# Attention and two mixtures on one core: the probability-value matmuls of a pair in two adjoining visits, with a padded last key chunk

## The chip, the cores and the metric

The kernel runs on one core of one Trainium2 chip. The metric is device time in microseconds (us): the median over runs, and beside it one execution that the hardware profiler recorded. TensorE (PE in the rows) multiplies matrices and transposes; VectorE (DVE), ScalarE (ACT) and GpSimd (POOL) do the rest; SyncE (SP) issues the loads. Each engine works through its own queue in order, and waits on semaphores for the others.

## The reference

Only the first of its three stages matters here, a block-causal attention over 4 batches, 8 heads, 576 positions of 64 values:

```python
scores = scale * np.matmul(q, k.transpose(0, 1, 3, 2))
mask = block_i >= block_j            # blocks of 64 positions, 9 of them
scores = np.where(mask, scores, -1000000000.0)
attn = np.exp(scores - np.max(scores, axis=-1, keepdims=True))
attn = attn / (np.sum(attn, axis=-1, keepdims=True) + 1e-09)
return np.matmul(attn, v).astype(np.float32)
```

A mixture of two dense layers over the 2304 tokens follows, and a second mixture with softmax routing through eight experts.

## The kernel before, in words

The attention works on 16 pairs (a batch and two heads that share the 128 partitions). For a pair the queries come in nine blocks of 64 rows; block b needs the 64(b+1) keys at or before it. Both heads of a block stand in one stationary matrix of 128 columns. The steps of a pair, each a method of class `Pair`, are: `lk`, `lq`, `lv` (loads on SyncE); `kh`, `kl`, `qh`, `ql`, `qs` (keys and scaled queries split in a high and a low part); `sc` (scores, five tiles of PSUM, with blocks 1 and 0, 3 and 2, 5 and 4, 7 and 6, and 8); `mx` (row maximum, VectorE, L145); `ex` (exponential and row sum, ScalarE, L149); `rs` (reciprocal of the sums); `no` (probabilities times the reciprocal, GpSimd, L160, in the tiles `pr`); `pt` (transposes of 128x128 pieces of the probabilities, TensorE, L169, up to four in one bank of PSUM); `pc` (copy of that bank to the tile `PT`, by ScalarE for `pc0`, `pc2`, `pc4`, `pc5`, `pc6` and by VectorE for `pc1`, `pc3`); `pv` (values times transposed probabilities, TensorE, L189); `xh`, `xl` (the result in two parts, to the next stage).

`pv` has seven steps: five key chunks of 128 for the query blocks 4 to 8 (`pv0` to `pv4`, 320, 320, 320, 192 and 64 columns, all summed in one bank "om"), and two for blocks 0 to 3 (`pv5`, `pv6`, 256 and 128 columns, in a bank "o"). Each step is a matmul per head with 64 columns of weights, and each of these two shows as two records. The last key chunk holds 64 keys: `pt6` transposes 64 columns, `pc6` copies 64 partitions, and `pv4` multiplies over 64 rows.

PSUM is held by two score tiles of two banks (`psc`), three banks for transposes and "o" (`ptr`), and one for "om" (`ppv`). A step that needs a tile waits until the last reader of the one it replaces is done.

The order of the work is written out by hand. `PLAN` is a list of steps run once per iteration `it`; the digit ahead of a step says how many pairs back it works: `5pv1` in iteration `it` is `pv1` of pair `it-5`. Each engine's queue is its part of that list, in that order; so TensorE's order is `3sc1 5pv1 5pv4 4pt5 3sc0 5pv5 5pv6 2sc3 3pt0 3pt1 4pv0 4pt6 2sc2 4pv3 3pt2 3pt3 2sc4 4pv2 3pt4`. Pairs 1 to 8 carry `w0`, `w1`, `w2` too, which load and split the first weights of the next stage. The tiles `QD`, `QF` and `pr` exist once for even and once for odd pairs and are zeroed where the steps never write, at the start, by GpSimd for the even and VectorE for the odd set (L248 to L256).

Of the kernel before, what the change touches and what calls it, by code (L numbers as in the profile page):

```python
# [7 lines left out]
F32 = mybir.dt.float32  # L8
# [6 lines left out]
P = 128  # L15
# [21 lines left out]
class Pair:  # L37
# [9 lines left out]
    def __init__(self, e, nc, b, p):  # L47
        self.e, self.nc, self.b, self.p = e, nc, b, p
        self.nm = f"{b}_{p}"
        self.ps, self.scs, self.om = {}, {}, {}  # L50
        self.eng = {**ENG, **START} if b + p == 0 else ENG
        i = (4 * b + p) % 2
        self.pr, self.QD, self.QF = e.pr[i], e.QD[i], e.QF[i]

    def step(self, name):
        getattr(self, name[:2])(*map(int, name[2:]))
# [12 lines left out]

    def lv(self):  # L70
        nc, src = self.nc, self.e.v[self.b, self.p]
        t = self.v = self.e.apool.tile([P, 5, 2, 64], F32, tag="natv", bufs=2, name=f"vn{self.nm}")
        nc.sync.dma_start(t[:, 0:4], src[0:512].rearrange("(c p) h d -> p c h d", p=P))
        nc.sync.dma_start(t[0:64, 4], src[512:576])

# [55 lines left out]
    def block(self, i):  # L131
        for u, b in enumerate(self.TILES[i]):
            if b < 8:
                yield b, self.scs[i][:, u, 0:64 * (b + 1)], self.pr[b][:, 0:64 * (b + 1)]
            else:
                yield b, self.scs[i][:, :, 0:288], self.pr[b].rearrange("p (a n) -> p a n", a=2)


    def mx(self, i):
# [23 lines left out]
    def pt(self, j):  # L163
        e, nc = self.e, self.nc
        ps = self.tr(f"p{j}")
        o, n = self.GROUPS[j]
        for u, (kc, b) in enumerate(self.CHUNKS[o:o + n]):
            m = P if kc < 4 else 64
            nc.tensor.transpose(ps[0:m, u * P:(u + 1) * P], self.pr[b][:, kc * P:kc * P + m], e.ident)  # L169

    def pc(self, j):
        ps = self.ps[f"p{j}"]
        if not hasattr(self, "PT"):
            self.PT = self.e.apool.tile([P, 25, 2, 64], F32, tag="PT", bufs=2, name=f"PT{self.nm}")
        o, n = self.GROUPS[j]
        m = P if j < 6 else 64
        self.e.copy(self.eng["pc"][j], self.PT[0:m, o:o + n].rearrange("p c h q -> p (c h q)"), ps[0:m, 0:n * P])


    def pv(self, j):  # L180
        e, nc = self.e, self.nc
        b0, b1, kc = self.PV[j]
        if kc == 0:
            self.om[b0] = e.ppv.tile([P, 512], F32, tag="pv", name=f"om{self.nm}") if b0 else self.tr("o")
        b = max(b0, 2 * kc)
        n = P if kc < 4 else 64
        c = self.CHUNKS.index((kc, b))
        for h in range(2):
            nc.tensor.matmul(self.om[b0][64 * h:64 * h + 64, (b - b0) * 64:(b1 - b0) * 64], self.v[0:n, kc, h, :],  # L189
                             self.PT[0:n, c:c + b1 - b, h, :], start=(kc == 0), stop=(kc == (b1 - 1) // 2))  # L190

    def xparts(self, a):
        b0, b1 = ((0, 4), (4, 9))[a]
# [15 lines left out]


PLAN = """
3sc1 2qh0 3mx4 5pv1 3rs0 4pc4 3mx1 3ex4 5pv4 2ql0 2ql1 4pc3 5xh1 1lq
2w2 4pt5 3ex1 3sc0 5xl1 3mx0 3no2 5pv5 5pv6 1qh1 3rs2 4pc5 5xh0 2qs0
2sc3 3no3 3pt0 3pt1 3ex0 1kh 3pc0 1w0 4pv0 5xl0 4pt6 3rs1 2mx3 3no4
2sc2 4pv3 4pc6 3pt2 3pc1 3no0 2mx2 1kl 3pt3 3lv 0lk 1w1 2ex3 2sc4
2qs1 3no1 3pc2 4pv2 3pt4 2ex2
"""
ENG = {"k": "A", "l": "P", "s": "DP", "q": "AA", "pc": "ADADAAA", "w": "P"}

# [10 lines left out]
def attention(e, tc, nb=4, wl=(1, 1 + 2 * READY)):  # L230
    nc = tc.nc
    e.ENG = ENG

    def copy(eng, dst, src):
        if eng == "A":
            nc.scalar.copy(dst, src)  # L236
        elif eng == "D":
            nc.vector.tensor_copy(dst, src)
        else:
            nc.gpsimd.tensor_scalar(out=dst, in0=src, scalar1=1.0, scalar2=1.0, op0=ALU.mult, op1=ALU.mult)  # L240
    e.copy = copy
    e.eng = lambda c: nc.vector if c == "D" else nc.gpsimd

    e.QD, e.QF, e.pr = [], [], []
    for i in range(2):
        e.QD.append(e.apool.tile([P, 2, 7, P], F32R, tag=f"QD{i}", bufs=1, name=f"QD{i}"))
        z = (nc.gpsimd, nc.vector)[i]
        z.memset(e.QD[i][0:64, :, :, 64:P].bitcast(F32), 0.0)  # L248
        z.memset(e.QD[i][64:P, :, :, 0:64].bitcast(F32), 0.0)
        e.QF.append(e.apool.tile([P, 2, P], F32, tag=f"QF{i}", bufs=1, name=f"QF{i}"))  # L250
        z.memset(e.QF[i][0:64, :, 64:P], 0.0)
        z.memset(e.QF[i][64:P, :, 0:64], 0.0)
        e.pr.append([e.apool.tile([P, min((b + 2) // 2 * P, 576)], F32, tag=f"pr{i}{b}", bufs=1, name=f"pr{i}{b}")
                     for b in range(9)])
        for b in range(0, 8, 2):
            z.memset(e.pr[i][b][:, 64 * (b + 1):], 0.0)  # L256
    pairs = [Pair(e, nc, b, p) for b in range(nb) for p in range(4)]
    n = len(pairs)
    plan = [(it - int(u[0]), u[1:]) for it in range(n + 6) for u in PLAN.split()]
    plan = [(i, u) for i, u in plan if (0 <= i < n if u[0] != "w" else wl[0] <= i < wl[1])]  # L260
    fill = [(int(u[0]), u[1:]) for u in FILL.split()]
    assert sorted(fill) == sorted(plan[:len(fill)])
    for i, u in fill + plan[len(fill):]:
        if u[0] != "w":
            pairs[i].step(u)
        else:
            t, c = (i - wl[0]) // 2, slice((i - wl[0]) % 2 * 256, (i - wl[0]) % 2 * 256 + 256)
            if u == "w0" and c.start == 0:
                e.moe.w_raw(t)
            elif u == "w1":  # L270
                e.moe.w_mul(t, c)
                for fn in e.moe.w_bits(t, c):
                    fn()
            elif u == "w2":
                for fn in e.moe.w_parts(t, c=c, eng=e.ENG["w"]):
                    fn()
# [647 lines left out]
def tile_attention_mixtures(ctx, tc, q, k, v, w_in, w_out, phi, w1, w2a, w2b, outa, outb):  # L924
# [25 lines left out]
    with tc.tile_pool(name="att", bufs=1, reuse_waits="tile") as e.apool:  # L950
        attention(e, tc)
        nc.sync.dma_start(e.phi, phi.rearrange("(k p) s -> p k s", p=P))
# [51 lines left out]
```

## Time and profile before

| | us |
|---|---|
| median of three runs | 683.61 (683.6 to 685.16) |
| the profiled execution's own time | 684.33 |
| its span | 682.3 |
| attention's end, first matmul of the next stage | 196.59 |

The span reaches from the first to the last instruction of the program; the execution's time holds a little more around it. A stretch of the steady attention holds the same work once per pair, so a period of it can be read like a loop. In a row of the chain of waits, the second number is the time for which that piece alone held up the end.

### The profile page before, as it was taken

The numbers are of one execution on the slowest core, as the hardware profiler recorded it, in microseconds if no ns is written. First come the engines' busy times: TensorE is split into PE (matmuls) and PEld (weight loads), VectorE is DVE, ScalarE is ACT, GpSimd is POOL, SyncE is SP. The second block draws the span as 40 slices with busy tenths as digits, with TensorE's granted clock in tenths as the row PEclk, the third lists the DMA queues.
The fourth block names the chain that finished last, engine by engine and source line by source line (L and its number), as shares of the span: only waits on it lengthen the run. The fifth ranks groups of instructions, "written<-read, shape, count | busy, mean of one in ns | idle before, by whom it ended". The sixth has DMA issues, their size and how long they took to land.

```text
span 682.3 us, 10701 instructions
## 1 busy us (share of the span) xinstructions
PE 662.7 (97%) x3903; PEld 504.1 (74%) x3903; DVE 417.0 (61%) x819; ACT 319.3 (47%) x774; POOL 307.2 (45%) x358
## 2 busy tenths in 40 slices
PE   7999999999998999999999999999999999988996
PEld 6777777777766888788888888888888877764344
DVE  7999887787747568675666566647533324533233
ACT  5888888888734434432333333323322232323223
POOL 4987875656415457555444553525622212210000
PEclk7899999999999999999999999999999999999898
DMA  4324231312030022111011201001321343459876
GB/s 152 120 84 133 56 105 53 106 53 70 23 141 31 32 79 106 62 32 35 28 61 32 93 31 63 0 32 32 122 94 61 124 155 123 155 189 325 320 309 278
DMA packets 31476, 69.96 MB, mean 103 GB/s; under 512 B 3392, under 2 KB 12736, under 8 KB 31424
## 3 DMA queue, kind: packets, MB, share of 16 engines
q1 hardware_dynamic: 31424, 69.28, 29.4%
q8 instruction: 31, 0.51, 0.3%
q14 instruction: 21, 0.17, 0.1%
HBM read 64.55 MB, written 4.72 MB: 102 GB/s over the span
## 4 chain that ended last, share of the span: by engine, by line
PE 90%; DVE 5%; ACT 3%; issue 1%; POOL 1%; DVEq 0%; ACTq 0%; POOLq 0%
PE h L405 28%; PE x L435 10%; PE x L436 9%; PE x L437 9%; PE sc L129 9%; PE om L189 7%; PE eh L788 2%; PE acc L816 2%; PE ps_3p L169 2%; PE ps_2p L169 2%; PE ps_1p L169 2%; PE ps_0p L169 2%; PE o L871 1%; PE x2t L528 1%; PE sc L121 1%
## 5 line engine op out<-in xcount | busy, mean ns | idle before, releaser
L405 PE MATMUL h<-xt,w 128*128 128x512 f32 (+1 forms) x960 | 215.0, 372 | 0.3 <-DVE ga L416 0.3
L419 POOL TENSOR_TENSOR g<-ga,g 128x512 fp32r<-128x512 f32 (+1 forms) x80 | 99.7, 1246 | 231.6 <-ACT g L418 202.2
L405 PEld LDWEIGHTS h<-xt,w 128*128 128x128 f32 x960 | 168.7, 188 | 34.9 <-issue 1.6
L414 DVE SCALAR_TENSOR_TENSOR ga<-ga 128x512 f32<-128x512 f32 (+1 forms) x80 | 66.7, 834 | 163.5 <-ACT ga L412 163.5
L435 PE MATMUL x<-w,g 128*128 128x512 f32 x288 | 115.8, 402 | 2.8 <-ACT x2p L236 2.8
L437 PE MATMUL x<-w,g 128*128 128x512 f32 x288 | 113.1, 393 | 0.0
L436 PE MATMUL x<-w,g 128*128 128x512 f32 x288 | 113.1, 393 | 0.0
L418 ACT CAST g<-ga 128x512 fp32r<-128x512 f32 (+1 forms) x80 | 46.3, 579 | 136.3 <-DVE ga L416 136.3
L160 POOL TENSOR_SCALAR pr<-pr,sm 128x384 f32<-128x384 f32 (+2 forms) x144 | 85.0, 606 | 48.3 <-DVE QF L99 25.4
L412 ACT ACTIVATE ga<-h,half 128x512 f32<-128x512 f32 (+1 forms) x80 | 51.7, 646 | 116.8 <-PE h L405 113.0
L129 PE MATMUL sc<-K,QD 128*128 128x288 f32 (+6 forms) x384 | 80.3, 347 | 3.9 <-ACT pr L149 1.7
L149 ACT ACTIVATE pr<-sc,nm 128x512 f32<-128x512 f32 (+2 forms) x144 | 75.2, 530 | 11.5 <-DVE nm L145 11.2
L145 DVE TENSOR_REDUCE nm<-sc 128x1 f32<-128x512 f32 (+2 forms) x144 | 63.9, 480 | 24.0 <-PE sc L129 23.8
L129 PEld LDWEIGHTS sc<-K,QD 128*128 128x128 f32 x384 | 61.7, 200 | 11.1 <-issue 3.7
L435 PEld LDWEIGHTS x<-w,g 128*128 128x128 f32 x288 | 54.2, 188 | 19.7 <-issue 4.6
L437 PEld LDWEIGHTS x<-w,g 128*128 128x128 f32 x288 | 54.2, 188 | 12.4
L436 PEld LDWEIGHTS x<-w,g 128*128 128x128 f32 x288 | 54.3, 189 | 10.6
L416 DVE TENSOR_TENSOR ga<-h,ga 128x512 f32<-128x512 f32 (+1 forms) x80 | 50.7, 634 | 1.9
L189 PE MATMUL om<-PT,vn 128*64 128x320 f32 (+2 forms) x320 | 48.9, 393 | 0.0
L354 POOL TENSOR_TENSOR wab<-wab,w 128x512 f32<-128x512 f32 (+1 forms) x36 | 43.6, 1212 | 10.1 <-ACT w L236 6.3
L355 POOL TENSOR_TENSOR w<-wab 128x512 fp32r<-128x512 f32 (+1 forms) x36 | 45.1, 1253 | 1.9
L447 DVE TENSOR_TENSOR x2p<-x,x2p 128x1024 f32<-128x1024 f32 (+1 forms) x32 | 37.0, 1182 | 1.0 <-PE x L437 0.8
(188 smaller groups left out, 735.4 us busy)
## 6 DMA issues: line engine op xcount, KB each, us to landing
ew<-in_w_dram SPq DMA_DIRECT2D x32, 512.0 KB, 4.5
raw<-in_w_in_dram SPq DMA_DIRECT2D x16, 512.0 KB, 3.3
raw<-in_w_out_dram SPq DMA_DIRECT2D x16, 512.0 KB, 3.4
ew<-in_w2a_dram SPq DMA_DIRECT2D x16, 510.0 KB, 6.2
ew<-in_w2b_dram SPq DMA_DIRECT2D x16, 344.0 KB, 7.4
kn<-in_k_dram SPq DMA_DIRECT2D x16, 288.0 KB, 3.9
qn<-in_q_dram SPq DMA_DIRECT2D x16, 288.0 KB, 4.0
vn<-in_v_dram SPq DMA_DIRECT2D x16, 256.0 KB, 2.8
```

Source lines behind the costliest of these rows:

```text
L129: nc.tensor.matmul(ps[:, 0:w], self.QD[:, qa, b - 2], self.K[:, ka, o:o + w], start=(k == 0), stop=(k == 2))
L145: nc.vector.tensor_reduce(out=self.negm[:, b:b + 1], in_=sc, axis=AX.XY if b == 8 else AX.X, op=ALU.max, negate=True)
L149: self.nc.scalar.activation(pr, sc, AF.Exp, bias=self.negm[:, b:b + 1], accum_out=self.sums[:, b:b + 1])
L160: self.nc.gpsimd.tensor_scalar(out=pr, in0=pr, scalar1=self.sums[:, b:b + 1], scalar2=1.0, op0=ALU.mult, op1=ALU.mult)
L169: nc.tensor.transpose(ps[0:m, u * P:(u + 1) * P], self.pr[b][:, kc * P:kc * P + m], e.ident)
L189: nc.tensor.matmul(self.om[b0][64 * h:64 * h + 64, (b - b0) * 64:(b1 - b0) * 64], self.v[0:n, kc, h, :], self.PT[0:n, c:c + b1 - b, h, :], ...
L405: nc.tensor.matmul(ph[:, 0:n], w[:, wi, kk], x[:, xi, 0:n], start=(m == 0), stop=(m == 11))
L414: nc.vector.scalar_tensor_tensor(out=ga, in0=ga, scalar=1.0, in1=ga, op0=ALU.min, op1=ALU.mult)
L419: nc.gpsimd.tensor_tensor(out=gl, in0=ga, in1=gh.bitcast(F32), op=ALU.subtract)
L435: nc.tensor.matmul(px, gh[:, c], w[:, 0], start=first, stop=False)
L436: nc.tensor.matmul(px, gh[:, c], w[:, 1], start=False, stop=False)
L437: nc.tensor.matmul(px, gl[:, c], w[:, 0], start=False, stop=last)
```

## The change

`pv0` to `pv4` of a pair become one step, `pa`, and `pv5`, `pv6` another, `pb`. In the new list both stand five pairs back, and between them there are only steps of other engines. The last chunk is padded: the tile `pr` of block 8 gets 640 columns, the last 64 of which are zeroed at the start; the value tile becomes a fixed one per even or odd pair whose partitions 64 to 127 of the last chunk are zeroed at the start; `pt6`, `pc6` and `pv4` then work on 128 keys. The list is reordered throughout, and the loads `lq` and `w0` are listed an iteration earlier. TensorE's order is now `4pt5 3sc1 5pa 5pb 3sc0 2sc3 3pt0 3pt1 2sc2 4pt6 3pt2 3pt3 2sc4 3pt4`.

```diff
--- before.py
+++ after.py
@@ -50,7 +50,7 @@
         self.ps, self.scs, self.om = {}, {}, {}
         self.eng = {**ENG, **START} if b + p == 0 else ENG
         i = (4 * b + p) % 2
-        self.pr, self.QD, self.QF = e.pr[i], e.QD[i], e.QF[i]
+        self.pr, self.QD, self.QF, self.v = e.pr[i], e.QD[i], e.QF[i], e.v_[i]
 
     def step(self, name):
         getattr(self, name[:2])(*map(int, name[2:]))
@@ -69,7 +69,7 @@
 
     def lv(self):
         nc, src = self.nc, self.e.v[self.b, self.p]
-        t = self.v = self.e.apool.tile([P, 5, 2, 64], F32, tag="natv", bufs=2, name=f"vn{self.nm}")
+        t = self.v
         nc.sync.dma_start(t[:, 0:4], src[0:512].rearrange("(c p) h d -> p c h d", p=P))
         nc.sync.dma_start(t[0:64, 4], src[512:576])
 
@@ -133,7 +133,7 @@
             if b < 8:
                 yield b, self.scs[i][:, u, 0:64 * (b + 1)], self.pr[b][:, 0:64 * (b + 1)]
             else:
-                yield b, self.scs[i][:, :, 0:288], self.pr[b].rearrange("p (a n) -> p a n", a=2)
+                yield b, self.scs[i][:, :, 0:288], self.pr[b][:, 0:576].rearrange("p (a n) -> p a n", a=2)
 
 
     def mx(self, i):
@@ -165,16 +165,14 @@
         ps = self.tr(f"p{j}")
         o, n = self.GROUPS[j]
         for u, (kc, b) in enumerate(self.CHUNKS[o:o + n]):
-            m = P if kc < 4 else 64
-            nc.tensor.transpose(ps[0:m, u * P:(u + 1) * P], self.pr[b][:, kc * P:kc * P + m], e.ident)
+            nc.tensor.transpose(ps[:, u * P:(u + 1) * P], self.pr[b][:, kc * P:(kc + 1) * P], e.ident)
 
     def pc(self, j):
         ps = self.ps[f"p{j}"]
         if not hasattr(self, "PT"):
             self.PT = self.e.apool.tile([P, 25, 2, 64], F32, tag="PT", bufs=2, name=f"PT{self.nm}")
         o, n = self.GROUPS[j]
-        m = P if j < 6 else 64
-        self.e.copy(self.eng["pc"][j], self.PT[0:m, o:o + n].rearrange("p c h q -> p (c h q)"), ps[0:m, 0:n * P])
+        self.e.copy(self.eng["pc"][j], self.PT[:, o:o + n].rearrange("p c h q -> p (c h q)"), ps[:, 0:n * P])
 
 
     def pv(self, j):
@@ -183,11 +181,18 @@
         if kc == 0:
             self.om[b0] = e.ppv.tile([P, 512], F32, tag="pv", name=f"om{self.nm}") if b0 else self.tr("o")
         b = max(b0, 2 * kc)
-        n = P if kc < 4 else 64
         c = self.CHUNKS.index((kc, b))
         for h in range(2):
-            nc.tensor.matmul(self.om[b0][64 * h:64 * h + 64, (b - b0) * 64:(b1 - b0) * 64], self.v[0:n, kc, h, :],
-                             self.PT[0:n, c:c + b1 - b, h, :], start=(kc == 0), stop=(kc == (b1 - 1) // 2))
+            nc.tensor.matmul(self.om[b0][64 * h:64 * h + 64, (b - b0) * 64:(b1 - b0) * 64], self.v[:, kc, h, :],
+                             self.PT[:, c:c + b1 - b, h, :], start=(kc == 0), stop=(kc == (b1 - 1) // 2))
+
+    def pa(self):
+        for j in range(5):
+            self.pv(j)
+
+    def pb(self):
+        for j in (5, 6):
+            self.pv(j)
 
     def xparts(self, a):
         b0, b1 = ((0, 4), (4, 9))[a]
@@ -209,11 +214,11 @@
 
 
 PLAN = """
-3sc1 2qh0 3mx4 5pv1 3rs0 4pc4 3mx1 3ex4 5pv4 2ql0 2ql1 4pc3 5xh1 1lq
-2w2 4pt5 3ex1 3sc0 5xl1 3mx0 3no2 5pv5 5pv6 1qh1 3rs2 4pc5 5xh0 2qs0
-2sc3 3no3 3pt0 3pt1 3ex0 1kh 3pc0 1w0 4pv0 5xl0 4pt6 3rs1 2mx3 3no4
-2sc2 4pv3 4pc6 3pt2 3pc1 3no0 2mx2 1kl 3pt3 3lv 0lk 1w1 2ex3 2sc4
-2qs1 3no1 3pc2 4pv2 3pt4 2ex2
+3ex2 4pc4 2w2 2qh0 3rs0 3no2 4pt5 3sc1 3ex4 5pa 3mx1 2ql1 2ql0 3rs2
+3ex1 5pb 4pc3 3no3 4pc5 2qs0 3sc0 2sc3 1kh 5xh1 5xl1 3mx0 1qh1 0lk
+5xh0 3pt0 5xl0 3ex0 3no4 0lq 3pc0 2mx3 3pt1 3rs1 2qs1 3pc1 3lv 2sc2
+2mx2 1w1 2ex3 4pt6 1kl 0w0 3pt2 3pt3 4pc6 2sc4 3pc2 3no0 3no1 3pt4
+2mx4
 """
 ENG = {"k": "A", "l": "P", "s": "DP", "q": "AA", "pc": "ADADAAA", "w": "P"}
 
@@ -241,7 +246,7 @@
     e.copy = copy
     e.eng = lambda c: nc.vector if c == "D" else nc.gpsimd
 
-    e.QD, e.QF, e.pr = [], [], []
+    e.QD, e.QF, e.pr, e.v_ = [], [], [], []
     for i in range(2):
         e.QD.append(e.apool.tile([P, 2, 7, P], F32R, tag=f"QD{i}", bufs=1, name=f"QD{i}"))
         z = (nc.gpsimd, nc.vector)[i]
@@ -250,10 +255,12 @@
         e.QF.append(e.apool.tile([P, 2, P], F32, tag=f"QF{i}", bufs=1, name=f"QF{i}"))
         z.memset(e.QF[i][0:64, :, 64:P], 0.0)
         z.memset(e.QF[i][64:P, :, 0:64], 0.0)
-        e.pr.append([e.apool.tile([P, min((b + 2) // 2 * P, 576)], F32, tag=f"pr{i}{b}", bufs=1, name=f"pr{i}{b}")
+        e.pr.append([e.apool.tile([P, (b + 2) // 2 * P], F32, tag=f"pr{i}{b}", bufs=1, name=f"pr{i}{b}")
                      for b in range(9)])
-        for b in range(0, 8, 2):
+        for b in range(0, 9, 2):
             z.memset(e.pr[i][b][:, 64 * (b + 1):], 0.0)
+        e.v_.append(e.apool.tile([P, 5, 2, 64], F32, tag=f"natv{i}", bufs=1, name=f"vn{i}"))
+        z.memset(e.v_[i][64:P, 4], 0.0)
     pairs = [Pair(e, nc, b, p) for b in range(nb) for p in range(4)]
     n = len(pairs)
     plan = [(it - int(u[0]), u[1:]) for it in range(n + 6) for u in PLAN.split()]
```

## Rows read from the trace of the kernel before

**Rows 1.** The page's part 1: each engine's busy us, share, instructions.

```profile
PE 662.7 (97%) x3903; PEld 504.1 (74%) x3903; DVE 417.0 (61%) x819; ACT 319.3 (47%) x774; POOL 307.2 (45%) x358
```

**Rows 2.** Stretches: start:end, us; then each engine's busy us, TensorE clock, DMA.

```profile
25.66:36.90 11.24, 10.23 (x71) 7.53 (x71) 9.97 (x27) 9.69 (x29) 10.41 (x17) 1.00 0.17 55
36.90:93.13 56.23, 56.23 (x408) 40.91 (x409) 50.85 (x135) 49.90 (x151) 45.92 (x70) 1.00 0.33 99
...
93.13:183.39 90.26, 90.22 (x651) 65.52 (x652) 70.51 (x184) 75.24 (x230) 53.52 (x90) 1.00 0.23 67
...
183.39:196.59 13.20, 13.20 (x108) 7.61 (x107) 5.59 (x19) 7.60 (x25) 4.04 (x8) 1.00 0.53 188
196.59:682.30 485.71, 472.07 (x2565) 364.84 (x2563) 259.99 (x407) 161.28 (x301) 178.38 (x144) 0.99 0.29 106
```

**Rows 3.** Chain of waits, one weight period: start us, us, what, instructions merged.

```profile
81.89 0.95 PE om L189 x8
82.84 0.59 PE ps_1p L169 x4
83.42 0.39 PE sc L121 x4
83.82 0.80 PE ps_0o L189 x8
84.62 1.50 PE sc L129 x6
86.12 0.87 PE ps_2p L169 x8
87.00 0.69 PE om L189 x4
87.69 0.23 PE ps_1p L169
87.92 0.98 PE sc L129 x6
88.89 0.48 PE om L189 x4
89.37 1.02 PE ps_2p L169 x8
90.39 0.80 PE sc L129 x6
91.19 0.69 PE om L189 x4
91.88 0.59 PE ps_2p L169 x4
92.46 0.67 PE sc L129 x6
```

**Rows 4.** Chain of waits in the drain of the attention.

```profile
194.04 1.81 PE om L189 x16
```

**Rows 5.** The page's part 5: groups, busy us, mean ns, idle before.

```profile
L149 ACT ACTIVATE pr<-sc,nm 128x512 f32<-128x512 f32 (+2 forms) x144 | 75.2, 530 | 11.5 <-DVE nm L145 11.2
L145 DVE TENSOR_REDUCE nm<-sc 128x1 f32<-128x512 f32 (+2 forms) x144 | 63.9, 480 | 24.0 <-PE sc L129 23.8
```

**Rows 6.** VectorE by line and shape, 36.90 to 93.13.

```profile
L107 DVE SCALAR_TENSOR_TENSOR QD<-qn,QD 64x448 fp32r<-64x448 f32 x10 | 8.2, 818 | 0.1
```

**Rows 7.** ScalarE by line and shape, 93.13 to 183.39.

```profile
L97 ACT ACTIVATE QD<-qn 64x448 fp32r<-64x448 f32 x14 | 8.0, 573 | 0.2
L149 ACT ACTIVATE pr<-sc,nm 128x576 f32<-128x576 f32 x9 | 6.7, 746 | 0.0
...
L236 ACT COPY PT<-ps_1p 128x512 f32<-128x512 f32 x8 | 4.7, 590 | 0.8 <-PE ps_1p L169 0.8
...
L236 ACT CAST K<-kn 128x576 fp32r<-128x576 f32 x7 | 4.7, 666 | 0.0
```

**Rows 8.** Chain of waits at the start of the kernel.

```profile
5.49 0.34 DVE pr L256 x4
```

## The prediction

> **What bounds the kernel now.** I read the page's busy shares first: TensorE is busy 97% of the span [rows 1]. A share over 682 us mixes three stages, so next come the stretches [rows 2]. From 36.90 to 183.39 us thirteen pairs of the attention pass one after another; TensorE is busy 146.45 of 146.49 us, at granted clock 1.00 (the 2.4 GHz level). Five of these periods (36.90 to 93.13, 11.25 us each) also prepare weights; there VectorE is busy 50.85/5 = 10.17 us a period, ScalarE 9.98, GpSimd 9.18. In the eight after them (11.28 us each) it is 8.81, 9.41 and 6.69. From 196.59 us the mixtures run, 485.7 us that the edit doesn't touch. The chain of waits decides whether "busy" is a bound: over one period it holds TensorE pieces alone, fifteen of them, end to end [rows 3]. So what shortens TensorE's own pieces shortens the period, until another engine takes over.
>
> **What a visit to the value matmuls costs.** In rows 3, "om" and "ps_0o" are visits to `pv`, "ps_1p/ps_2p" transposes, "sc" scores. A `pv` step is four records. Four of 320 columns take 0.69 us, four of 192 columns 0.48: 0.41 ns a column and 0.165 us that no column explains, the price of going in. Going out shows in the next piece: eight transposes after scores take 0.87 (0.109 each), after `pv` 1.02; four take 0.59 instead of 0.44; so 0.15. Scores: `sc2` (2112 columns) 0.98 and `sc1` (1344) 0.67, both after transposes, give 0.40 ns a column and 0.13 fixed; `sc3` (2880) would then be 1.29 and takes 1.50 behind `pv`: 0.21. A round trip is 0.32 to 0.37 us, and there are five in a period. The 0.95 of `pv1`+`pv4` (1536 columns, 0.63) holds 0.165 for going in and 0.155 more for the last chunk's 64 rows. One row checks this: in the drain four steps follow each other without a piece between, 3584 columns in 1.81 us [rows 4]; 0.165+1.47+0.155 is 1.79.
>
> A rule of the Trainium skill stands here, "TensorEngine Tiling (Array Packing)", Key Properties: a change of tiling mode, not of tile alone, drains the TensorE; "TensorE: Matmul & The Clock Gate" (phase 4, drain) puts the drain at about 128 cycles, an estimated 0.05 us at full clock. The rows agree that a switch costs something, but show 0.15 to 0.21 each way. By the pages' figure four round trips are 0.43 us a period, and the whole change would end near 679 us.
>
> **The change, part by part.**
> 1. One visit. On TensorE's queue nothing stands between `5pa` and `5pb` (what is listed between belongs to VectorE, ScalarE and GpSimd), so the two are one visit of 6400 columns: 0.165+2.62 = 2.79 us. Before, the five took 3.61, and what followed them paid the exits.
> 2. Zero padding. `pv4` becomes a 128-row step and its 0.155 goes. The one transpose of `pt6` goes from 64 to 128 columns: at most 0.109, and it now joins `pt2`. `pc6` copies 128 partitions instead of 64, at the same elements per partition: between 0 and 0.3 us of ScalarE (half of a 512-column copy's 0.59 [rows 7]); I take 0.
> 3. The new period on TensorE, in queue order: `pt4`+`pt5` 0.87, `sc1` 0.67, values 2.79, `sc0` 0.39+0.15, `sc3` 1.29, `pt0`+`pt1` 0.87, `sc2` 0.98, `pt6`+`pt2`+`pt3` 9 x 0.109 = 0.98, `sc4` 0.80. Sum 9.79, against 11.25. The row does not show `sc0` before `sc3`; a switch there costs 0 to 0.21. I take 9.9 with hand-overs.
> 4. Can the others follow? During the 2.79 us visit no score tile is produced. ScalarE has queued for it the exponentials of tile 4 (0.75) and tile 1 (two, 0.53 each by the mean [rows 5]), a copy (0.59), `kh` (0.67) and `qh1` (0.57) [rows 7]: 3.6 us, so it covers. VectorE has `mx1` (two at 0.48), two `ql` (0.82 each [rows 6]), `rs2` and a copy: over 3 us. In the eight plain periods the next largest load is ScalarE's 9.41, so TensorE still sets 9.9. In the five weight periods VectorE's 10.17 plus gaps between dependent instructions is above TensorE's 9.9; between 10.17 and 11.25 I take 10.4.
> 5. Queues. `0lk`, `0lq` and `0w0` reach SyncE one slot earlier or later; `0lk` still waits for the score step `3sc0`, which frees its buffer, and `3lv` stands behind it, with two periods until `5pa` needs the values. Now `lv` is also held by `5pb` of the pair two before, done earlier in the same slot. No cost while that lead holds; if it went, a period's transposes would stall a landing time.
> 6. Start. Two more memsets per VectorE/GpSimd set (pr block 8, value tile). Four such took 0.34 us and lie on the chain of waits at 5.49 [rows 8]: 0.085 to 0.3 us more; I take 0.2.
> 7. The first value period. 25.66 to 36.90 held three visits of pair 0 which now all come later. VectorE's 9.97 then decides: -0.9, bounds 0 to -1.1.
> 8. Drain. Values of the last two pairs come later in the plan. 183.39 to 196.59 is 13.20 us of saturated TensorE. By the same pieces the new one holds 6.8+3.5+2.9 = 13.2 us and ends in three long visits, each behind copies (ScalarE is busy 7.60 of 13.20, so it waits too): +0.1 to +3; I take +1.3.
>
> **Sum.** Plain periods 8 x 9.9 = 79.2 against 90.26: -11.1. Weight periods 5 x 10.4 = 52.0 against 56.23: -4.2. First value period -0.9, drain +1.3, start +0.2. Together -14.7 on the profiled execution's 684.33 us (span 682.3, the rest lies around it): 669.6. That execution is 0.7 above the median 683.61 of the runs, so I forecast 669. Its own range: all bounds kind (9.79, 10.17, -1.1, +0.1, +0.1) give -18.2, or 665.4; 10.2, 10.9, 0, +3 and +0.3 give -7.1, or 676.5.
>
> **Rivals.**
> A. The score buffers limit (chance 0.19). Two hold five tiles a period. Writing takes 4.34 us (the sc pieces of rows 3), reducing 9 x 0.48, exponentials 9 x 0.53 [rows 5]: 13.4 us, 6.7 a buffer. If a buffer comes free during the visit it stays empty for 2.79: 9.5; each exponential behind a 0.59 copy adds up to 1.5: 11.0. At 10.6 in plain and 10.9 in weight periods, drain +2, the sum is -5.2: about 678. For it: the visit is four times as long as the longest before. Against: in rows 3 TensorE never waited, and item 4 covers it.
> B. The pages' drain (0.05): -0.43 a period in 13, drain +1, start +0.2: about 679.
> C. The cost is in the weight loads of `pv`, not the switching (0.05): the pieces keep their length wherever they stand, and the drain and start remain: 685. Against: rows 4.
> D. Slower (0.06). The three transpose buffers. `5pb` takes one while `pt3`'s and `pt5`'s contents still wait for `4pc3` and `4pc5`, so `3pt0` and `3pt1` wait for VectorE's `pc3`, which stands behind `mx1`, two `ql` and `rs2`. That is 0.96+1.64+0.3+0.69 = 3.6 us after `sc1`; TensorE arrives after 2.79+0.54+1.29 = 4.6. Covered by 1 us; but if VectorE reaches `mx1` late by 2.5 or more, TensorE loses what the one visit won. It decides from 1.46 us of wait a period; at 2.0, 13 x 0.54 plus drain and start gives 693.
>
> **How the numbers follow.** Forecast 0.65, A 0.19, B 0.05, C 0.05, D 0.06. A difference under 0.3% (2 us) can't be told from none. Faster: forecast, A, B: 0.89. Within 0.3%: C: 0.05. Slower: 0.06. The range 665 to 679 holds the forecast's own range and most of A and B.
>
> **What would show it.** The chain of waits over one plain period still TensorE alone, 9.8 to 10.0 us long, with one "om" piece of about 2.8 (the short visit's records behind it, no transposes or scores between), transposes at 0.109 throughout, `sc3` near 1.29, no 64*64 records. Weight periods near 10.4 with TensorE waiting for VectorE's copies. The forecast is wrong if TensorE waits for ScalarE or VectorE in the plain periods (A, D), if the long visit takes above 3.3 (C), or if the mixtures' 485.7 us change.

## The result, and the profile after

The changed kernel takes 673.68 us, median of four runs (672.87 to 674.39), against 684.38 (683.6 to 685.43) for the kernel before, timed beside it: ratio 0.9842, 95% interval 0.982 to 0.9865. The forecast was 669, the range 665 to 679: faster, as predicted, by 10.7 us of the 14.7 in the sum. The profiled execution took 674.28 us, its span is 672.5; before, 684.33 and 682.3.

Page, part 1 of the changed kernel (each engine's busy us, share, instructions), against [rows 1]:

```profile
PE 647.0 (96%) x3903; PEld 507.3 (75%) x3903; DVE 417.2 (62%) x821; ACT 316.4 (47%) x774; POOL 308.7 (46%) x360
```

TensorE is busy 15.7 us less with the same 3903 matmuls; the others' busy times change by 3 us at most. Stretches of the changed kernel, cut at the same places as [rows 2] (start:end, us, then busy time of TensorE, its weight loads, VectorE, ScalarE, GpSimd, clock, DMA):

```profile
36.82:89.59 52.77, 52.52 (x406) 42.79 (x405) 51.08 (x136) 48.74 (x151) 45.23 (x71) 1.00 0.35 105
89.59:172.09 82.50, 82.45 (x650) 68.62 (x649) 69.32 (x187) 74.45 (x231) 56.60 (x90) 1.00 0.24 73
172.09:186.32 14.23, 12.82 (x116) 8.85 (x115) 5.43 (x18) 7.15 (x25) 4.37 (x9) 1.00 0.48 174
186.32:672.50 486.18, 472.14 (x2565) 364.81 (x2563) 260.30 (x407) 161.12 (x301) 178.14 (x144) 0.99 0.29 105
```

Line by line against [rows 2]: the five weight periods 56.23 to 52.77 (10.55 each), the next eight 90.26 to 82.50 (one still 10.55, seven 10.28), the drain 13.20 to 14.23. The start ends where it did (36.90, now 36.82), and the mixtures, whose code is unchanged, take 486.18 for 485.71. The attention ends at 186.32 instead of 196.59: 10.27 us, of which 9.8 are left in the span. The mixtures run the same code in every kernel here, and their stretch is between 484.5 and 487.3 us long in the profiled executions shown; so differences of 1 to 3 us are read below from the periods and from the attention's end, not from the medians. The granted clock in the attention is 1.00 in both, the 2.4 GHz level, so no clock is in this sum.

The chain of waits over one plain period of the changed kernel (start us, us, what, instructions merged):

```profile
110.52 2.21 PE om L186 x20
112.73 0.65 PE ps_3o L186 x8
113.38 0.59 PE sc L121 x4
113.97 1.37 PE sc L129 x6
115.33 0.87 PE ps_1p L168 x8
116.21 0.98 PE sc L129 x6
...
117.29 0.88 PE ps_1p L168 x8
118.17 1.03 PE sc L129 x6
119.20 0.87 PE ps_1p L168 x8
120.08 0.72 PE sc L129 x6
120.80 2.21 PE om L186 x20
```

TensorE alone, 10.28 us from one long visit to the next, one visit to the value matmuls (2.21 + 0.65 = 2.86) where [rows 3] has five, transposes at 0.109 each, and no extra 0.15 in any of them. The one piece out of line is `sc4` at 118.17: 1.03, although the same six matmuls took 0.80 in [rows 3]. The waits of the plain periods say why (engine and line, what it waited for, us in total, times, longest):

```profile
PEld sc L129 <- ACT pr L149: 1.2, 6, 0.2
```

Once a period the weight load of `sc4` waits 0.2 us for an exponential, `ex3`, to empty one of the two score buffers. The weight periods are another thing. Their chain, a few of its pieces (same columns):

```profile
79.61 0.57 DVE nm L145 x2
...
80.21 0.88 DVE QD L107
...
81.13 0.84 DVE QD L107
...
82.14 0.67 DVE PT L243
```

There VectorE has become the bound, as item 4 of the prediction had it.

### The profile page after: what moved, and what is told of

Read it like the earlier page. It is cut to its first block, busy times and chain, and to the rows that moved or that the text cites. A ratio compares the mean times of both kernels' runs of the same rounds, so it can differ in the third digit from the quotient of the medians.

```text
span 672.5 us, 10671 instructions
## 1 busy us (share of the span) xinstructions
PE 647.0 (96%) x3903; PEld 507.3 (75%) x3903; DVE 417.2 (62%) x821; ACT 316.4 (47%) x774; POOL 308.7 (46%) x360
## 4 chain that ended last, share of the span: by engine, by line
PE 79%; DVE 14%; ACT 3%; issue 2%; POOL 1%; DMA 1%; SPq 0%; DVEq 0%; ACTq 0%; POOLq 0%
PE h L412 28%; PE x L442 10%; PE x L443 9%; PE x L444 9%; PE sc L129 5%; DVE nm L145 4%; PE om L186 3%; PE eh L795 2%; PE acc L823 2%; DVE QD L107 2%; DVE PT L243 1%; POOL pr L160 1%; PE o L878 1%; PE ps_0p L168 1%; PE x2t L535 1%
## 5 line engine op out<-in xcount | busy, mean ns | idle before, releaser
L129 PEld LDWEIGHTS sc<-K,QD 128*128 128x128 f32 x384 | 59.2, 192 | 15.1 <-ACT pr L149 6.7
L186 PE MATMUL om<-PT,vn 128*64 128x320 f32 (+2 forms) x320 | 36.4, 374 | 0.5 <-ACT PT L241 0.5
```

The lines of the kernel that those rows point to most:

```text
L129: nc.tensor.matmul(ps[:, 0:w], self.QD[:, qa, b - 2], self.K[:, ka, o:o + w], start=(k == 0), stop=(k == 2))
```

## The experiments

**1. The visits joined in the old order, without the padding.** Only the places of the value steps in the plan change:

```diff
-... 5pv1 ... 5pv4 ... 5pv5 5pv6 ... 4pv0 ... 4pv3 ... 4pv2
+... 5pa  ...          5pb
```

> The kernel before with the five steps pv0 to pv4 joined at the place of 5pv1 and pv5, pv6 kept where they are, no padding, nothing else moved: two visits a period instead of five. Theory (the switches in and out of the value matmuls are the cost): three round trips of 0.32 us go, so a plain period falls from 11.28 to about 10.3 and a weight period to about 10.6; near 674 us. Rival (the new order of the other steps is what pays, joining alone meets new waits): plain periods of 11.0 or more, 680 us or more.

Measured: 687.98 us (ratio 1.0057, 1.0039 to 1.0076). The periods are 11.56 to 11.58, one 11.85, longer than before. Chain of one of them, and from its waits (us in total, times, longest) the one that matters:

```profile
104.33 2.38 PE om L189 x20
...
106.73 0.49 ACT xt L211 x2
107.22 0.87 ACT pr L149 x4
...
108.11 0.58 ACT QD L97
...
108.71 0.59 ACT PT L244
```

```profile
ACT xt L211 <- PE om L189: 1.7, 1, 1.7
```

`5xh1` (L211) reads what the long visit writes. In the old order it stands on ScalarE's queue ahead of `ex1`, so ScalarE stands still for 1.7 us while the visit runs, and the period then goes through the queue behind it. As the rival expected, joining alone doesn't bring the gain; the kernel gets slower: the reordering isn't a side issue of the change but the condition for it. The new order with five visits was not run; by the chain in [rows 3], TensorE's own pieces alone would still fill 11.25 us of its period, or 11.11 with the padding (experiment 3).

**2. The same, with the consumers' copies moved.** `5xh1` goes next to `5xh0`, `5xl1` next to `5xl0`, behind work that is ready:

```diff
-... 4pc3 5xh1 1lq 2w2 4pt5 3ex1 3sc0 5xl1 3mx0 ... 4pc5 5xh0 ... 1w0 5xl0
+... 4pc3 1lq 2w2 4pt5 3ex1 3sc0 3mx0 ... 4pc5 5xh1 5xh0 ... 1w0 5xl1 5xl0
```

> join_old with one thing moved: the copies out of the long visit, xh1 on ScalarE and xl1 on VectorE, listed beside xh0 and xl0 instead of ahead of ex1. Theory (in join_old ScalarE stands at xh1 for 1.7 us a period until the long visit ends, while the exponentials behind it are ready): the plain period falls from 11.58 to 10.4 to 10.7, the whole to 675 to 679. Rival (the score tiles are out of buffers during a long visit, whatever ScalarE's order): it stays at 11.2 or more.

Measured: 682.06 (ratio 0.9972, 0.9949 to 0.9994), plain periods 10.95, weight periods 11.08. The wait of experiment 1 is gone, but the period didn't come down to TensorE's own sum. Chain:

```profile
112.23 2.35 PE om L189 x20
...
118.42 0.75 ACT PT L244 x2
...
119.25 1.39 ACT pr L149 x4
120.64 0.48 ACT PT L244
121.12 1.09 ACT pr L149 x4
...
122.25 0.93 PE sc L129 x6
```

From the transposes on, a ring over ScalarE's copies and exponentials holds TensorE. So the theory was right on the wait and wrong on the size, and the period lies between it (10.4 to 10.7) and the rival (11.2 or more): of the 1.04 us between experiment 1 and the whole new order (10.54, experiment 4), two moves bring 0.63.

**3. The padding alone, with the old plan.**

```diff
-3ex2 4pc4 2w2 2qh0 3rs0 3no2 4pt5 3sc1 3ex4 5pa ...
+3sc1 2qh0 3mx4 5pv1 3rs0 4pc4 3mx1 3ex4 5pv4 ...   (all five lines as before)
```

> The changed kernel with the old list of steps: five visits, old order, padding alone. Theory: the 0.155 us of the 64-row step go, 0.05 come back in the longer transpose, so 0.1 a period and about 1 to 2 us in all: 682.5 to 683.5. Rival (padding is what pays): 10 us. Rival (padding pays nothing): 684.4, no change.

Measured: 685.21 (ratio 1.0014, 0.9991 to 1.0037), plain periods 11.24, as before. The visit of `pv1` and `pv4` falls from 0.95 [rows 3] to 0.80, the 0.155 of item 2, and `sc4` takes 0.91 for 0.80. Why, is seen in the timeline of one plain period (start us, us, engine, line, operation, shapes): the transposes `pt2` and `pt3`, the last part of the exponential `ex3`, and `sc4`, in the kernel before,

```profile
157.06 1.09 PE L169 MATMUL ps_0p<-ident,pr 128*128 128x128 f32 x8
157.64 0.20 ACT L149 ACTIVATION_READ_ACCUMULATOR pr<-sc,nm 128x1 f32 x1
157.91 1.03 PE L129 MATMUL sc<-K,QD 128*128 128x288 f32 x6
```

and with the padding:

```profile
157.61 1.09 PE L168 MATMUL ps_0p<-ident,pr 128*128 128x128 f32 x8
158.30 0.20 ACT L149 ACTIVATION_READ_ACCUMULATOR pr<-sc,nm 128x1 f32 x1
158.55 1.06 PE L129 MATMUL sc<-K,QD 128*128 128x288 f32 x6
```

Before, `sc4` starts 0.85 us after the first of the eight transposes, and 0.07 after `ex3` has emptied a score buffer (157.84). With the padding it starts 0.94 after them, and 0.05 after `ex3` (158.50): TensorE now waits for ScalarE. `ex3` itself waits for VectorE's maxima (0.57 us in this period) and VectorE for scores, and the last four plain periods are 11.24 each: a ring over three engines. As far as this run stands for the kernel before, that ring is right behind TensorE's 11.25 there. Its chain of waits showed such a wait in one of thirteen periods only: from 115.61 to 127.16, 11.55 long, where `sc4` took 1.06. TensorE's own need with the padding is 11.11: three of the first six periods have that length, and there `sc4` takes 0.79.

The whole is a balance, too. The thirteen periods together take 146.16 for 146.49, and the drain is 0.54 shorter; but the first of them starts at 37.88 instead of 36.90. The attention ends at 196.70, as before. The padding is worth next to nothing in the old order; what it is worth in the new one, experiment 4 says.

**4. The changed kernel without the padding** (64 keys in the last chunk again):

```diff
-tensor.transpose(ps[:, u*P:(u+1)*P], self.pr[b][:, kc*P:(kc+1)*P], ...)
+m = P if kc < 4 else 64
+tensor.transpose(ps[0:m, u*P:(u+1)*P], self.pr[b][:, kc*P:kc*P+m], ...)
```

> The changed kernel with a last chunk of 64 keys again (64 columns transposed, 64 partitions copied, 64 rows multiplied), in the new order. Theory: the 64-row step inside the long visit costs a switch on both sides, so a plain period rises from 10.28 by 0.15 to 0.25 and the whole by 1.5 to 3 us, 675 to 677. Rival (the padding does nothing inside a visit): 673.7.

Measured: 678.09 (ratio 0.99, 0.9858 to 0.9942), plain periods 10.54, the attention's end 188.73, 2.4 us later than in the changed kernel, as the theory had it; the medians differ by 4.4. Chain:

```profile
110.58 2.35 PE om L189 x20
112.94 0.80 PE ps_3o L189 x8
113.74 0.59 PE sc L121 x4
```

2.35 and 0.80 against 2.21 and 0.65: the 64-key step costs 0.15 on either side of the border in the visit. In the new order, where TensorE decides, the padding is worth 0.26 of each plain period; in the old it was worth 0.01. And the new order without it still takes 0.7 off each period (10.54 for 11.25): the larger part of the gain doesn't hang on the padding.

**5. The changed kernel with two visits** (`5pb` behind `3pt0`, and its copies moved accordingly):

```diff
-3ex1 5pb 4pc3 ... 5xh0 3pt0 5xl0 3ex0 3no4 0lq 3pc0 2mx3 3pt1 ...
+3ex1 4pc3 ... 3pt0 5pb 3ex0 5xh0 3no4 0lq 3pc0 2mx3 5xl0 3pt1 ...
```

> The changed kernel with the short step pb moved behind 3pt0 (xh0 and xl0 behind it in turn), so that scores and transposes part the two visits. Theory: one round trip more, plain periods 10.28 + 0.32 = 10.6, weight periods, which VectorE sets, 10.55 to 10.7: 2.5 to 4 us more, 676 to 678. Rival (plain periods are set by hand-overs, not by TensorE's own pieces): no change, 673 to 675.

Measured: 676.1 (ratio 0.9879, 0.9843 to 0.9916), plain periods 10.30, weight periods 10.64, the attention's end 187.11, 0.8 us later than in the changed kernel. Chain:

```profile
115.39 0.80 PE ps_3o L186 x8
116.19 0.59 PE ps_1p L168 x4
...
118.74 0.79 PE sc L129 x6
```

The price of the second visit is there, 0.15 going in (0.80 for 0.65) and 0.15 coming out (0.59 for 0.44). But `sc4` falls from 1.03 to 0.79: the TensorE that comes later finds the score buffer free. The period is 0.02 longer, not 0.30: the mechanism is right, the theory's size is not, and the period comes out as the rival said. (The median falls in the theory's range; but of its 2.4 us, only 0.8 are the attention's.) So the last round trip that the change saves is worth almost nothing here, because the wait at `sc4` stands behind it.

**6. Another order at the start** (`1kh` of the second pair behind its `1w1`):

```diff
-FILL = ""
+FILL = """... 1qh1 2lk 2lq 0mx3 0qs1 0sc2 0mx2 1w1 1kh 0ex3 1kl 2w0 0sc4 0mx4"""
```

> The changed kernel, with the first three iterations listed so that ScalarE's kh of the second pair comes behind its w1, so that GpSimd's kl of that pair no longer runs beside VectorE's kl of the first. Theory (the two share a way to memory: VectorE's kl took 1.94 us beside GpSimd's, 0.76 alone): kl is back at 0.76, the first full score tile starts near 8.8 instead of 9.95, and the attention ends about 1 us earlier, 672.7 in all. Rival (the waits before the first value visit swallow it): the first visit still starts at 36.8 us and nothing is gained.

The collision that this takes away, in the timeline of the changed kernel (start us, us, engine, line, operation, shapes, idle time before in brackets):

```profile
6.56 1.41 POOL L83 TENSOR_TENSOR K<-kn,K 128x576 fp32r<-128x576 f32 x1 [2.20 <-ACT K L241]
6.65 1.94 DVE L83 TENSOR_TENSOR K<-kn,K 128x576 fp32r<-128x576 f32 x1
```

and with the other order:

```profile
6.64 0.76 DVE L83 TENSOR_TENSOR K<-kn,K 128x576 fp32r<-128x576 f32 x1
...
9.77 1.41 POOL L83 TENSOR_TENSOR K<-kn,K 128x576 fp32r<-128x576 f32 x1 [5.40 <-ACT K L241]
```

VectorE's subtraction waits out GpSimd's, which ends at 7.97, and ends 0.62 us later. The Trainium skill, "SBUF — State Buffer", section "SBUF: two separate sides", calls the port pair of these two engines an exclusive lock for operations with two SBUF inputs, held for the whole instruction: the trace agrees. The first full visit comes at 35.53 instead of 36.82 and the attention ends at 185.00 instead of 186.32; the median, 673.44 (672.89 to 673.88; ratio 0.9843, 0.9809 to 0.9877), can't tell that from the changed kernel. It is the earliest end of an attention with the whole computation in this study.

**7. A tile of its own for each block's row maximum.** The idea: `ex3`'s first exponential waits for the tile of nine maxima, not for its own.

```diff
-self.negm = ap.tile([P, 9], F32, tag="negm", ...)
+self.negm = [ap.tile([P, 1], F32, tag=f"negm{b}", ...) for b in range(9)]
```

> The changed kernel with a tile of its own for each block's row maximum instead of nine columns of one tile. Theory (the first exponential of a score tile starts only behind the second reduction of that tile, 0.3 to 0.6 us after its own, because both write one tile): ex3 starts 0.4 us earlier, the 0.2 us for which sc4 waits for ex3 go, and a plain period falls from 10.28 to 10.05 to 10.15; 1.5 us in all. Rival (the exponential waits for another reason, or sc4 for another): no change.

Measured: 674.05 (ratio 0.9848, 0.9813 to 0.9884), plain periods 10.27: nothing. Timeline of `ex3`:

```profile
116.61 0.69 ACT L149 ACTIVATE pr<-sc,nm 128x512 f32<-128x512 f32 x1 [0.24 <-DVE sm L154]
117.29 0.63 ACT L149 ACTIVATE pr<-sc,nm 128x448 f32<-128x448 f32 x1
```

The first still starts only when both maxima of its score tile are done (115.30 + 1.22 = 116.52), the second doesn't wait. So the shared tile wasn't the cause. Whether `ex3` waits for the second maximum or for VectorE's next operation, the `sm` that the row names (it ends at 116.60), no run tells apart; it is worth at most the 0.24.

**8. One of VectorE's four operations on the weights** in `w1`, three left out:

```diff
-for fn in e.moe.w_bits(t, c):
+for fn in e.moe.w_bits(t, c)[2:3]:
```

> The changed kernel without three of VectorE's four operations of w1 in the attention (the first weights of the next stage are then wrong). Theory (VectorE sets the weight periods): they fall from 10.55 to the plain period's 10.28, six of them, 1.6 us. Rival (GpSimd's or ScalarE's share of the weight work sets them): they stay at 10.5.

Measured: 672.68 (ratio 0.9832, 0.9778 to 0.9887). A weight period as a stretch (columns as above):

```profile
46.34:56.62 10.28, 10.28 (x83) 8.58 (x82) 9.37 (x25) 9.71 (x32) 9.04 (x14) 1.00 0.30 93
```

10.28 instead of 10.55, the same as a plain one: VectorE sets the weight periods, and with less work gives back 0.27 a period.

**9. A shorter exponential in `ex3`**, 64 of block 6's 448 columns:

```diff
+if b == 6:
+    sc, pr = sc[:, 0:64], pr[:, 0:64]
```

> The changed kernel with the exponential of block 6, the last that sc4 waits for, cut from 448 to 64 columns (the probabilities of block 6 are then wrong), 0.38 us of ScalarE. Theory (in a plain period TensorE's own pieces are 10.07 us and 0.2 us are its wait at sc4 for ex3): sc4 falls from 1.00 to 0.80 us and the plain period from 10.28 to 10.05 to 10.1. Rival (ScalarE's whole load sets the plain period): it falls by the 0.38 us taken away, to 9.9. Rival (TensorE's own pieces are all of it): it stays at 10.28.

Measured: 673.34 (ratio 0.9839, 0.9787 to 0.989), plain periods 10.00. Chain:

```profile
108.40 0.79 PE sc L129 x6
109.19 0.87 PE ps_0p L170 x8
110.06 0.68 PE sc L129 x6
```

`sc4` is back at 0.79, and no wait of TensorE for an exponential is left in the plain periods. 10.00 is therefore what TensorE needs by itself, and 0.28 of the changed kernel's 10.28 hang on `ex3`: 0.24 as the wait at `sc4`, the rest at `sc1` (0.72, now 0.68).

**10. Both `qs` operations on GpSimd**, to relieve VectorE in the weight periods, and **11. the same on top of experiment 6**, as a candidate for the best version:

```diff
-ENG = {..., "s": "DP", ...}
+ENG = {..., "s": "PP", ...}
```

> The changed kernel with qs of both heads on GpSimd instead of one on VectorE. Theory (VectorE sets the weight periods, and its qs holds it for 0.40 us there): they fall from 10.55 to 10.28 to 10.35, the plain periods stay at 10.28; 1.2 to 1.6 us earlier at the attention's end. Rival (the second qs holds up GpSimd's normalisation and TensorE waits for that): the weight periods stay at 10.5 or rise.

> start_fix and qs_pool together. Theory: their gains add, 1.3 us at the start and 1.2 to 1.6 us in the weight periods: the attention ends near 183.5 us, 671 in all, 2 to 3 us under the changed kernel. Rival (one gain swallows the other): 672.5 to 673.5.

Measured: 676.73 (ratio 0.9888, 0.9834 to 0.9942) and 675.77 (0.987, 0.9839 to 0.9902); weight periods 10.84 and 10.85 instead of 10.55, plain ones 10.28; the attention ends at 188.68 and 186.90. A weight period has, in the changed kernel and then in experiment 10:

```profile
52.69 1.42 POOL L83 TENSOR_TENSOR K<-kn,K 128x576 fp32r<-128x576 f32 x1
53.74 0.39 DVE L154 TENSOR_SCALAR sm<-sm 128x4 f32<-128x4 f32 x1
```

```profile
54.01 1.43 POOL L83 TENSOR_TENSOR K<-kn,K 128x576 fp32r<-128x576 f32 x1
54.53 0.93 DVE L154 TENSOR_SCALAR sm<-sm 128x4 f32<-128x4 f32 x1
```

The second `qs` stands on GpSimd's queue ahead of the subtraction `kl`, which so comes later against VectorE's `rs`. The first operation of `rs` takes 0.16 us in a plain period, where nothing of GpSimd's runs beside it; here it ends 0.02 us behind GpSimd's subtraction in both kernels, and takes 0.39 in the one, 0.93 in the other. So VectorE, rid of a `qs` of 0.49, loses 0.54 again in waiting, and TensorE's wait for VectorE's copies of the transposes rises from 0.2 to 0.8 or 0.9 a period. How the two add up to 0.29 stays open. Neither kernel beats the changed one.

## Why the prediction was right, and where its sizes were off

- **The mechanism held.** A switch of TensorE between value matmuls and other work has a price of its own, about 0.15 going in and 0.15 coming out (experiment 5), and so has the 64-key step, 0.15 a side (experiment 4). Rivals B (a price of 0.05) and C (the price is in the weight loads) fall by that: under C both experiments would have left the pieces as long as they were. Rival D didn't come: there is no wait for `pc3` at `3pt0` or `3pt1`. The drain of the Trainium skill, "TensorE: Matmul & The Clock Gate" (phase 4, drain), about 128 cycles or an estimated 0.05 us, is a third of what these rows show.
- **Items 1 and 2** (2.79 us for the one visit; padding free): 2.86, and `pc6` takes 0.26 as before.
- **Item 3, the plain period, was mis-sized:** taken 9.9 (pieces 9.79), measured 10.28. Pieces by themselves need 10.00 (experiment 9): the visit, `sc0` and `sc3` took 0.05 to 0.08 more each than their parts summed up from [rows 3]. The other 0.28 is the wait for `ex3`, nearly all at `sc4`: rival A's mechanism, in one place, at 0.28 instead of the 0.7 that A put on it. By the prediction's own last sentence (wrong if TensorE waits for ScalarE in the plain periods) this counts against it: the path was TensorE's own but for this wait. The prediction covered the time of the long visit with ScalarE's queue, but not the moment half a period later when both score buffers are full. Over the eight periods this is the largest miss, -7.76 for -11.1; 0.27 of it is that the first of the eight is still a weight period.
- **Item 4** (VectorE sets the weight periods, 10.4): right by experiment 8, 10.55; -3.46 for -4.2. Its claim that the others follow is true only of the new order: joined in the old one, the period is 11.58 (experiment 1).
- **Items 6 and 7, the start:** +0.2 and -0.9 foreseen, nothing in the sum. The first full score tile moved from 8.15 to 9.95, 1.8 us later; of this, 0.47 comes with the memsets (experiment 3, which has them in the old order, starts that tile at 8.62), over the 0.3 that item 6 allowed, and 1.2 is the collision of experiment 6, which the prediction didn't look for. The first value period then made good what the start had lost.
- **Item 8, the drain:** +1.3 foreseen, +1.03.
- **Item 5**, the queues: no wait on a load was seen in the stretches.

By terms, in us: plain periods 3.3 short, weight periods 0.7, start 0.6, drain 0.3 better, mixtures 0.5 longer: 4.9 of the span, 14.7 to 9.8.

## What to carry to other kernels

A chain of waits that shows one engine alone says that this engine is the bound, not by how much: here a second ring was some 0.01 us behind it in a period of 11.25 (experiment 3), so find the next ring (take a little off the first engine, and see whether the period follows) before pricing a saving there. When work is joined into one long visit, everything on in-order queues that consumes its result must move behind work that is ready, or it stops the queue for the length of the visit. And a saved piece is worth its length only up to the next wait: the last round trip cost 0.30 in its pieces and 0.02 in the period.

## What the runs showed of the hardware that was not expected

Switching TensorE cost 0.15 us each way, the same for a change of tile width (128 to 64 columns) as for one of depth (128 to 64 rows), so that multiplying by 64 rows of zeros is cheaper for TensorE than leaving them out. What the 0.15 is made of, no run takes apart. Two subtractions of 128x576, one on VectorE and one on GpSimd, ran one after the other, not side by side: 0.76 alone, 1.94 for the one that started second. Even a VectorE operation on 128x4 elements, 0.16 alone, took 0.93 beside such a subtraction (experiment 10). And the spans of one and the same program differed by several us with the mean granted clock: among runs of the kernel before, 680.1 us at 0.992 and 685.6 at 0.981, with the attention at 1.00 in every stretch shown; so a gain of 1 us in the attention (experiment 6) is seen in the trace and not in a median.
